# One core, an attention, channel-mixing and expert kernel: the order in which expert weights are fetched at the start of the expert stage

## The chip, the core and the metric

The kernel runs on one core of a Trainium2 chip. The metric is device microseconds of one execution. The core has five engines, each with its own in-order instruction stream: TensorE (PE in the profile, with its weight loads as PEld), VectorE (DVE), ScalarE (ACT), GpSimd (POOL) and SyncE (SP). SP computes nothing here; it issues the large transfers from DRAM, one after the other, and waits in between wherever a buffer is not free. The rows of gathered tokens and of results go through POOL's own transfer queue.

## What is computed

Three layers follow one another on 2 x 768 tokens of width 512: chunked attention with a few memory rows, a channel-mixing layer, and a mixture of 8 experts. The change touches the third alone. Cut to what matters:

```python
for b in range(B):
    prev_e = -1
    for s in range(S):
        fresh_e = int(np.argmax(logits[b, s]))
        e = fresh_e if s == 0 or local_gate[b, s] < 0.5 or prev_e < 0 else prev_e
        prev_e = e
        p = softmax(logits[b, s])
        h = np.maximum(x[b, s] @ w1[e], 0.0)      # w1: 8 x 512 x 1024
        out[b, s] = p[e] * (h @ w2[e])            # w2: 8 x 1024 x 512
```

Each token goes to one expert, and which one is known only on the chip. One expert's weights are two matrices of 2,048 KB each.

## The kernel before

**Slots.** The tokens of one expert are cut into full slots of 128 rows; what is left of an expert's tokens, if it is at most 64, becomes a half slot of 64 rows. Full slots run in order of their experts, numbered from 0; half slot h runs behind the full slot `HALF_AT[h]`, with `HALF_AT = (3, 5, 7, 8, 9, 11, 13, 15)`, so the first half slot stands behind full slot 3, which is the fourth, and the second behind full slot 5. With these inputs there are eleven full slots and five half slots. Full slots 0 to 3 belong to one expert, 4 to 7 to a second, 8 to a third, 9 and 10 to a fourth.

**Weights of full slots.** There is one raw buffer for them, `raw[0]`, in two halves: `raw[0][0]` for w1 and `raw[0][1]` for w2. `w_fetch(s, k)` (lines 848 to 855) has SP load half k of the next expert's weights into it when slot s is the first of an expert, and otherwise issues an empty load: the same instruction with a condition that is false. Either way it first reads two numbers of the table `nx` into SP's registers. `w_part(s, q)` (lines 835 to 846) turns a quarter of the raw weights into two lists of high and low parts: ACT writes the high part (line 830) and DVE subtracts it (line 833), four pieces each; it runs only if slot s is the first of its expert. For slot s + 1 its first two quarters run inside slot s, between the two middle parts of the second product (lines 1178 and 1180), the other two in slot s + 1 (lines 1161 and 1167).

**Weights of half slots.** They are used as they are, from `raw[1]` for half slots 0, 2, 4 and `raw[2]` for 1, 3, 5. `h_fetch(h)` (lines 1088 to 1096) reads two numbers of the table `ei` and issues two loads, r1 (line 1095) and r2 (line 1096). `half_end(h)` fetches for half slot h + 2 once half slot h has been computed.

**The order around the change.** Before slot 1, SP issues in this order (lines 1234 to 1238): a tiny transfer `mark`, which waits for the gather of slot 2; half slot 0's two loads; the second expert's two loads (`w_fetch(0, 0)` and `w_fetch(0, 1)`); half slot 1's two loads. Then come the `w_fetch` calls of slots 1 to 3: (2,0), (2,1), (3,0) and (3,1), which are empty here since slots 2 and 3 start no expert, and (4,0), which is a load of the third expert's w1 and needs `raw[0][0]` free. The framework makes every load, empty ones too, wait for the load that wrote the same half before it, and for its readers; and it makes a reader wait for the last load in program order, whether that was empty or not. So `w_part(4, 0)`, in slot 3, waits for the empty `w_fetch(3, 0)`.

**The first half slot.** On ACT the order in slot 3 is `w_part(4, 0)` (line 830), the high part of the next slot's transposed tokens (line 865), `w_part(4, 1)` (line 830), the scaling of slot 3's result `put` (line 909), and then half slot 0's first activation `h_relu(0)` (line 1121). On TensorE it is slot 3's last products, half slot 0's first product (line 1115), the transpose of its result (line 1128, which needs the activation of line 1121), the rest of the first product, the second product (line 1140, which needs r2), and slot 4's first product (line 882).

Of the kernel before, what the change touches and what calls it, by code (L numbers as in the profile page):

```python
# [143 lines left out]
def kernel(  # L144
# [692 lines left out]
    def w_part(s, part):  # L837
        if s < 2 or s >= NFULL:
            return
        k = (s, body[0] if s > NMIN and body[0] >= NMIN else 0)  # L840
        if k not in flag:
            flag[k] = nc.values_load(ei[0:1, 1, s:s + 1], engines=(ET.DVE, ET.Activation),
                                     min_val=0, max_val=1)
        with tc.If(flag[k]):  # L844
            for c in range(4):
                w_piece(s, part, c, nc.vector)

    def w_fetch(s, k):

        if s >= NFULL:  # L850
            return
        ev = nc.values_load(nx[0:1, 0, s:s + 1], engines=(ET.SP,), min_val=0, max_val=NE - 1)
        fv = nc.values_load(nx[0:1, 1, s:s + 1], engines=(ET.SP,), min_val=0, max_val=1)
        nc.sync.dma_start(out=raw[0][k], in_=(w1, w2)[k][bass.ds(ev, 1)].rearrange("o (c p) f -> p (o c) f", p=P),
                          cond=fv)

    def gather(s):
        if s >= NFULL:
            return
        rows = 1 + (NE_T * P if s < 2 else B * S)  # L860
        nc.gpsimd.indirect_dma_start(out=yg[s % 3], out_offset=None, in_=ys[0:rows, :],
                                     in_offset=bass.IndirectOffsetOnAxis(ap=gix[:, s:s + 1], axis=0))
# [5 lines left out]
    def tx(s):  # L868
        if s >= NFULL:
            return  # L870
        pb = banks[4]
        for c in range(NC):
            nc.tensor.transpose(pb[:, c * P:(c + 1) * P], yg[s % 3][:, c * P:(c + 1) * P], ident)
        split4(pb, *xbuf[s % 2])

    def s1(s, g, cs):
        xh, xl = xbuf[s % 2]
        pb = banks[g]
        for c in cs:
            wh, wl = w1_s[c][g]  # L880
            sl = slice(c * P, (c + 1) * P)
            nc.tensor.matmul(pb, lhsT=xh[:, sl], rhs=wh, start=(c == 0), stop=False)  # L882
            nc.tensor.matmul(pb, lhsT=xh[:, sl], rhs=wl, start=False, stop=False)  # L883
            nc.tensor.matmul(pb, lhsT=xl[:, sl], rhs=wh, start=False, stop=(c == NC - 1))  # L884

    def relu(s, g, on_act):
        if on_act:
            nc.scalar.activation(out=hv[g], in_=banks[g], func=ACTF.Relu)
        else:
            nc.vector.tensor_scalar(out=hv[g], in0=banks[g], scalar1=0.0, scalar2=None, op0=ALU.max)  # L890

    def th(s, g):
        pb = banks[5]
        for c in range(4):
            nc.tensor.transpose(pb[:, c * P:(c + 1) * P], hv[g][:, c * P:(c + 1) * P], ident)  # L895
        split4(pb, *hbuf[g])

    def s2(s, cs):
        pb = banks[2 + s % 2]
        for c in cs:  # L900
            hh, hl = hbuf[c // 4]
            wh, wl = w2_s[c]
            sl = slice((c % 4) * P, (c % 4 + 1) * P)
            nc.tensor.matmul(pb, lhsT=hh[:, sl], rhs=wh, start=(c == 0), stop=False)  # L904
            nc.tensor.matmul(pb, lhsT=hh[:, sl], rhs=wl, start=False, stop=False)  # L905
            nc.tensor.matmul(pb, lhsT=hl[:, sl], rhs=wh, start=False, stop=(c == NF - 1))  # L906

    def put(s):
        nc.scalar.activation(out=ot[0], in_=banks[2 + s % 2], func=ACTF.Copy, scale=yg[s % 3][:, DM:DM + 1])
        nc.vector.tensor_copy(sixl, six[:, s:s + 1])  # L910

    def store():

        nc.gpsimd.indirect_dma_start(out=out, out_offset=bass.IndirectOffsetOnAxis(ap=sixl, axis=0),  # L914
                                     in_=ot[0], in_offset=None, bounds_check=B * S - 1, oob_is_err=False)
# [172 lines left out]
    def h_fetch(h):  # L1088
        if h >= NE:
            return  # L1090
        s = NFULL + h
        ev = nc.values_load(ei[0:1, 0, s:s + 1], engines=(ET.SP,), min_val=0, max_val=NE - 1)
        fv = nc.values_load(ei[0:1, 1, s:s + 1], engines=(ET.SP,), min_val=0, max_val=1)
        r1, r2 = raw[1 + h % 2]
        nc.sync.dma_start(out=r1, in_=w1[bass.ds(ev, 1)].rearrange("o (c p) f -> p (o c) f", p=P), cond=fv)
        nc.sync.dma_start(out=r2, in_=w2[bass.ds(ev, 1)].rearrange("o (c p) f -> p (o c) f", p=P), cond=fv)
# [6 lines left out]
    def h_tx(h):  # L1103
        if h >= NE:
            return
        pb = banks[6]
        for c in range(NC):
            nc.tensor.transpose(pb[:, c * 64:(c + 1) * 64], yh[h % 2][0:64, c * P:(c + 1) * P], ident[0:64, 0:64])
        nc.scalar.activation(out=xh4[h % 2], in_=pb[:, 0:256], func=ACTF.Copy)
# [47 lines left out]
    def slot_body(s):  # L1157
        body[0] = s
        if s > 1:
            s1(s, 0, range(4))  # L1160
            w_part(s, 2)
            relu(s, 0, True)
        s1(s, 1, range(0, 2))
        th(s, 0)
        s1(s, 1, range(2, 4))
        relu(s, 1, False)
        w_part(s, 3)
        if s > 1:
            w_fetch(s, 1)
        if s - 1 not in HALF_AT:  # L1170
            store()
        gather(s + 2)
        s2(s, range(0, 2))
        if s in HALF_AT:
            h_tx(HALF_AT.index(s))
        th(s, 1)
        s2(s, range(2, 4))
        w_part(s + 1, 0)
        tx(s + 1)
        w_part(s + 1, 1)  # L1180
        if s > 0:
            w_fetch(s + 1, 0)
        s2(s, range(4, 8))
        put(s)

# [20 lines left out]
    def slots(s):  # L1206
        slot_body(s)
        if s == 1:
            h_gather(0)
            h_gather(1)  # L1210
            for k in range(2):
                nc.gpsimd.memset(oh[k], 0.0)
        if s in HALF_AT:
            with tc.If(nh > HALF_AT.index(s)):
                half_body(HALF_AT.index(s))
            store()
            half_end(HALF_AT.index(s))
        if s < NMIN - 1:
            slots(s + 1)
        elif s < NFULL - 1:  # L1220
            with tc.If(nv > s + 1):
                slots(s + 1)
# [9 lines left out]


    nc.sync.dma_start(out=mark, in_=yg[2][0:1, 0:1])
    h_fetch(0)
    w_fetch(0, 0)
    w_fetch(0, 1)
    h_fetch(1)
    slots(1)
    nr = nc.values_load(ei[0:1, 0, NSLOT + 2:NSLOT + 3], min_val=0, max_val=1)  # L1240
    with tc.If(nr):
# [83 lines left out]
```

## Time and profile before

| | us |
|---|---|
| median of 3 runs | 464.93 (464.39 to 465.23) |
| the profiled execution | 464.7 |
| its span in the trace | 462.9 |
| around the span | 1.8 |

The span is the time from the first to the last instruction of the program that the profiler saw. TensorE is busy for 90% of it. The expert stage with its slots runs from about 245 us to the end. In a timeline a row is a run of like instructions: its start, its length, engine and line, the operation with what it writes and reads, the number of instructions, and in square brackets how long the engine sat idle before it and what ended that. SPq marks instructions of SP; for a transfer the time is that of issuing it, not of moving it.

### The profile page before, as it was taken

Reading aid. Unit: us, or ns where it says so; the run is one execution under the profiler, and the core shown is the slowest. Engines: PE = TensorE matmul, PEld = TensorE weight load, DVE = VectorE, ACT = ScalarE, POOL = GpSimd, SP = SyncE. Lnnn points to the kernel's source line nnn. Section 1 sums busy time; section 2 is a strip of 40 time slices with the busy share of each in tenths; the row PEclk is TensorE's granted clock in tenths of the full one; section 3 lists DMA queues with packets and bytes.
Section 4 is the critical chain, followed back from the end, with each engine's and each line's share of the span. In section 5 each row is a group of like instructions: output and inputs, shape, how many; then the busy total and the mean of one; then the engine's idle time right before and its main releaser. Section 6 shows DMA issues by size and latency. Waiting matters only on the chain. (4 is left out here: it accounts for less than half of the span.)

```text
span 462.9 us, 10040 instructions
## 1 busy us (share of the span) xinstructions
PE 416.2 (90%) x3827; PEld 351.1 (76%) x3827; DVE 251.8 (54%) x637; ACT 186.8 (40%) x425; POOL 95.2 (21%) x98
## 2 busy tenths in 40 slices
PE   0557999999999999999999899994999999999992
PEld 0346899988999989998999678872686786767671
DVE  4999999735664476548622684214242116475210
ACT  3664995355420634214624212215332125465211
POOL 2312211422200221003313505110320210212020
PEclk9999999999999999999999999998899999999997
DMA  8979950224221120000750015999992850994010
GB/s 283 408 295 330 372 171 6 67 75 133 89 87 36 47 60 1 1 1 25 278 178 0 1 68 152 390 400 357 378 385 81 274 209 1 355 392 139 23 53 25
DMA packets 28099, 76.68 MB, mean 166 GB/s; under 512 B 3821, under 2 KB 3953, under 8 KB 28034
## 3 DMA queue, kind: packets, MB, share of 16 engines
q1 hardware_dynamic: 25218, 67.39, 40.1%
q0 software_dynamic: 2816, 8.47, 5.7%
q8 instruction: 34, 0.56, 0.5%
q14 instruction: 31, 0.25, 0.2%
HBM read 109.40 MB, written 6.69 MB: 251 GB/s over the span
## 5 line engine op out<-in xcount | busy, mean ns | idle before, releaser
L866 DVE TENSOR_TENSOR w<-bank,w 128x512 fp32r<-128x512 f32 x34 | 23.5, 690 | 72.8 <-ACTq L844 56.8
L212 POOL TENSOR_TENSOR k2l<-tmp,k2h 128x384 fp32r<-128x384 f32 x25 | 28.4, 1135 | 100.9 <-DVE k2h L209 63.8
L480 PE MATMUL bank<-xkh,w 128*128 128x384 f32 x128 | 46.6, 364 | 1.7 <-ACT tmp L500 1.6
L833 DVE TENSOR_TENSOR w<-raw,w 128x512 fp32r<-128x512 f32 x56 | 35.7, 696 | 19.7 <-ACT w L830 19.3
L481 PE MATMUL bank<-xkl,w 128*128 128x384 f32 x128 | 43.7, 341 | 1.0 <-DVE xkl L212 1.0
L480 PE MATMUL bank<-k2h,w 128*128 128x384 f32 x128 | 44.6, 349 | 0.0
L482 PE MATMUL bank<-xkh,w 128*128 128x384 f32 x128 | 43.7, 341 | 0.0
L482 PE MATMUL bank<-k2h,w 128*128 128x384 f32 x128 | 42.9, 335 | 0.0
L481 PE MATMUL bank<-k2l,w 128*128 128x384 f32 x128 | 42.8, 334 | 0.0
L865 ACT ACTIVATE w<-bank 128x512 fp32r<-128x512 f32 x34 | 20.3, 597 | 52.0 <-PE bank L895 27.8
L830 ACT ACTIVATE w<-raw 128x512 fp32r<-128x512 f32 x64 | 35.2, 621 | 8.2 <-DMA raw<-in_w_dram 8.2
L904 PE MATMUL bank<-w,w 128*128 128x512 f32 x88 | 36.3, 412 | 0.0
L882 PE MATMUL bank<-w,w 128*128 128x512 f32 x88 | 36.2, 412 | 0.0
L906 PE MATMUL bank<-w,w 128*128 128x512 f32 x88 | 34.6, 393 | 0.0
L883 PE MATMUL bank<-w,w 128*128 128x512 f32 x88 | 34.6, 393 | 0.0
L884 PE MATMUL bank<-w,w 128*128 128x512 f32 x88 | 34.6, 393 | 0.0
L905 PE MATMUL bank<-w,w 128*128 128x512 f32 x88 | 34.3, 390 | 0.0
L914 POOL DMA_INDIRECT out_dram<-ot,sixl x11 | 11.2, 1018 | 104.5 <-ACTq L844 29.5
L382 ACT ACTIVATE Pm<-bank,mx 128x64 f32<-128x64 f32 x96 | 21.3, 321 | 21.8 <-DVE mx L373 21.2
L506 ACT ACTIVATE tmp<-bank 128x384 f32<-128x384 f32 x24 | 11.9, 494 | 41.5 <-PE bank L482 38.9
L480 PEld LDWEIGHTS bank<-xkh,w 128*128 128x128 f32 x128 | 24.6, 192 | 4.7 <-ACT tmp L500 2.0
L481 PEld LDWEIGHTS bank<-xkl,w 128*128 128x128 f32 x128 | 24.6, 192 | 1.4 <-DVE xkl L212 1.4
(224 smaller groups left out, 916.7 us busy)
## 6 DMA issues: line engine op xcount, KB each, us to landing
raw<-in_w_dram SPq DMA_DIRECT2D x36, 2048.0 KB
qk<-in_qkx_dram SPq DMA_DIRECT2D x16, 576.0 KB
vt<-in_vx_dram SPq DMA_DIRECT2D x16, 390.0 KB
w<-in_wk_dram SPq DMA_DIRECT2D x8, 512.0 KB
w<-in_wv_dram SPq DMA_DIRECT2D x8, 512.0 KB
ys<-yr SPq DMA_DIRECT2D x12, 256.0 KB
w<-in_wr_dram SPq DMA_DIRECT2D x4, 512.0 KB
raw<-in_w_dram SPq DMA_DIRECT2D x2, 1024.0 KB
```

The source lines that it names most:

```text
L212: (nc.vector if e == "d" else nc.gpsimd).tensor_tensor(out=o, in0=a, in1=b, op=op)
L480: nc.tensor.matmul(o[:, :UT], lhsT=wh, rhs=xh, start=first, stop=False)
L481: nc.tensor.matmul(o[:, :UT], lhsT=wh, rhs=xl, start=False, stop=False)
L482: nc.tensor.matmul(o[:, :UT], lhsT=wl, rhs=xh, start=False, stop=last)
L830: nc.scalar.activation(out=hi, in_=src, func=ACTF.Copy)
L833: lo_on.tensor_tensor(out=lo, in0=src, in1=hi.bitcast(F32), op=ALU.subtract)
L882: nc.tensor.matmul(pb, lhsT=xh[:, sl], rhs=wh, start=(c == 0), stop=False)
L883: nc.tensor.matmul(pb, lhsT=xh[:, sl], rhs=wl, start=False, stop=False)
L884: nc.tensor.matmul(pb, lhsT=xl[:, sl], rhs=wh, start=False, stop=(c == NC - 1))
L904: nc.tensor.matmul(pb, lhsT=hh[:, sl], rhs=wh, start=(c == 0), stop=False)
L905: nc.tensor.matmul(pb, lhsT=hh[:, sl], rhs=wl, start=False, stop=False)
L906: nc.tensor.matmul(pb, lhsT=hl[:, sl], rhs=wh, start=False, stop=(c == NF - 1))
```

## The change

Before slot 1 the next expert's two loads are issued first and half slot 0's two behind them; half slot 1's two loads are not issued there any more. They are issued in slot 3, right behind `w_fetch(4, 0)`. No instruction of another engine changes, and the number of loads and their sizes stay the same.

```diff
@@ slot_body
         w_part(s + 1, 1)
         if s > 0:
             w_fetch(s + 1, 0)
+        if s == 3:
+            h_fetch(1)
         s2(s, range(4, 8))
         put(s)
@@ ahead of slot 1
     nc.sync.dma_start(out=mark, in_=yg[2][0:1, 0:1])
-    h_fetch(0)
     w_fetch(0, 0)
     w_fetch(0, 1)
-    h_fetch(1)
+    h_fetch(0)
     slots(1)
```

## Rows read from the trace of the kernel before

**Rows 1.** The page: busy time by engine, and the span in 40 equal slices.
```profile
PE 416.2 (90%) x3827; PEld 351.1 (76%) x3827; DVE 251.8 (54%) x637; ACT 186.8 (40%) x425; POOL 95.2 (21%) x98
PE   0557999999999999999999899994999999999992
```
**Rows 2.** Timeline of PE, half slot 0 to slot 4: start, length, engine, line.
```profile
313.40 2.81 PE L1115 MATMUL bank<-raw,xh 128*64 128x256 f32 x24
322.13 0.69 PE L1128 MATMUL bank<-ident,hv 128*128 128x128 f32 x2 [5.92 <-ACT hv L1121]
330.11 0.50 PE L882 MATMUL bank<-w,w 128*128 128x512 f32 x1
```
**Rows 3.** Timeline of ACT, slot 3 and half slot 0.
```profile
308.98 0.60 ACT L865 ACTIVATE w<-bank 128x512 fp32r<-128x512 f32 x1 [0.81 <-PE bank L895]
316.48 2.19 ACT L830 ACTIVATE w<-raw 128x512 fp32r<-128x512 f32 x4 [6.91 <-DMA raw<-in_w_dram]
...
321.70 0.37 ACT L1121 ACTIVATE hv<-bank 128x256 f32<-128x256 f32 x1
```
**Rows 4.** Timeline of SP (issues): the first loads, then the empty ones.
```profile
282.16 0.29 SPq L1234 DMA_DIRECT2D mark<-yg  x1
286.10 0.01 SPq L1095 DMA_DIRECT2D raw<-in_w_dram  x1
286.36 0.39 SPq L1096 DMA_DIRECT2D raw<-in_w_dram  x1
288.26 4.45 SPq L854 DMA_DIRECT2D raw<-in_w_dram  x1
...
314.28 0.08 SPq L854 DMA_DIRECT2D raw<-in_w_dram  x1
316.34 0.08 SPq L854 DMA_DIRECT2D raw<-in_w_dram  x1
...
322.78 0.38 SPq L854 DMA_DIRECT2D raw<-in_w_dram  x1
```
**Rows 5.** SP's waits, 306 to 316.5 us: total, times, longest.
```profile
SPq L854 <- DMA raw<-in_w_dram: 3.5, 1, 3.5
```
**Rows 6.** Stretches: length, busy time by engine, granted clock, DMA share, GB/s.
```profile
286.00:314.10 28.10, 27.63 (x139) 22.23 (x139) 5.53 (x10) 5.95 (x10) 3.98 (x4) 1.00 1.01 374
314.10:322.80 8.70, 2.78 (x24) 1.49 (x20) 5.57 (x10) 5.59 (x11) 0.00 (x0) 0.90 1.02 389
318.00:320.00 2.00, 0.00 (x0) 0.00 (x0) 2.00 (x4) 2.00 (x5) 0.00 (x0) 1.00 1.05 387
322.00:327.00 5.00, 4.87 (x22) 2.30 (x22) 1.14 (x4) 0.46 (x2) 1.02 (x1) 0.50 0.72 230
```
**Rows 7.** Timeline of PE, half slot 2, behind slot 7.
```profile
389.98 2.81 PE L1115 MATMUL bank<-raw,xh 128*64 128x256 f32 x24
392.72 0.44 PE L1128 MATMUL bank<-ident,hv 128*128 128x128 f32 x2
394.00 1.03 PE L1140 MATMUL bank<-raw,hh 128*64 128x256 f32 x8
398.07 0.50 PE L882 MATMUL bank<-w,w 128*128 128x512 f32 x1
```
**Rows 8.** Timeline of ACT, slot 7 and half slot 2; one row of slot 8.
```profile
386.09 2.20 ACT L830 ACTIVATE w<-raw 128x512 fp32r<-128x512 f32 x4
...
392.03 0.39 ACT L1121 ACTIVATE hv<-bank 128x256 f32<-128x256 f32 x1 [0.61 <-PE bank L1115]
...
398.62 2.20 ACT L830 ACTIVATE w<-raw 128x512 fp32r<-128x512 f32 x4
```
**Rows 9.** Timeline of DVE: the table `nx`; the low parts in slot 7.
```profile
276.12 0.15 DVE L1047 CAST nx<-tmp 1x17 int32<-1x17 f32 x1
390.12 2.48 DVE L833 TENSOR_TENSOR w<-raw,w 128x512 fp32r<-128x512 f32 x4
```
**Rows 10.** Timeline of PE, the start of half slot 1.
```profile
356.02 2.81 PE L1115 MATMUL bank<-raw,xh 128*64 128x256 f32 x24
```

## The prediction

> **What bounds the kernel now.** I read the page first: TensorE is busy for 90% of the span, and in the row of 40 slices it stands at 9 from the fourth or fifth slice to the end, but for one slice of 4, the 28th (312 to 324 us), one of 8 and the last [rows 1]. So the expert stage is bound by TensorE, and the one hole is worth a look of its own. The timeline of PE shows it: the first product of half slot 0 starts at 313.40, and the transpose behind it at 322.13, after 5.92 us idle that ended with ACT's activation of line 1121 [rows 2]. Then the timeline of ACT tells why that came late. ACT was done with slot 3's previous piece at 308.98 + 0.60 = 309.58, stood idle for 6.91 us until a load into `raw`, and then did, in its order, w_part(4, 0) from 316.48, the rest, and the activation at 321.70, ended 322.07 [rows 3]. That is 5.59 us of ACT work behind the wait, and half slot 0's activation is queued behind all of it, though it needs nothing of it.
>
> Which load was it? The order of issues on SP answers: the third `w_fetch` of the empty ones, (3, 0), goes out at 316.34, and ACT starts 0.14 us later [rows 3, 4]. It was late because the one before it, (2, 1), had to wait for the load that wrote `raw[0][1]` before it: SP waited 3.5 us for a transfer [rows 5] and issued (2, 1) at 314.28 and (3, 0) 2.06 us later [rows 4]. The load that it waited for is `w_fetch(0, 1)`, fourth in SP's queue, which therefore landed at about 314.1. From the first issue at 286.10 that is 28.0 us for four loads [rows 4], 7.0 us each, at 374 GB/s with the gathers and stores in between [rows 6].
>
> **What the change removes.** Without the wait, slot 3 and half slot 0 should look like slot 7 and half slot 2, where the same instructions run in the same order with w_part(8, 0) and (8, 1) in front of the activation. There ACT starts w_part at 386.09, 3.89 us before PE's first product at 389.98; the same distance from 313.40 is 309.51, when ACT is free in slot 3 too [rows 3, 7, 8]. There the transpose starts 2.74 us after the first product and slot 8 follows 8.09 us after it [rows 7]. In slot 3 these are 8.73 and 16.71 us [rows 2]. So 16.71 - 8.09 = **8.62 us** go: 5.99 of stall, and 2.63 of slow clock behind it. [...]
>
> **When the new order releases w_part(4, 0).** `nx` is written at 276.12 [rows 9], before `mark` goes out at 282.16 [rows 4], so the table is no new wait. From the end of one issue to a `w_fetch`'s own it takes 288.26 - 286.75 = 1.51 us to read the two numbers [rows 4]. The first load of the new order, `w_fetch(0, 0)`, can go out at 282.45 + 1.51 = 284.0; at the latest I take 286.3, if whatever held SP until 286.10 holds it again. `w_fetch(0, 1)` is now second instead of fourth: landed after 2 x 7.0 = 14.0 us, at 298.0 to 300.3; were the second to land only when three have their share, 21 us after the first issue, 307.3. Add 2.06 us for (3, 0): w_part(4, 0) is released at 300.1 to 302.4, and at 309.4 by the far bound. ACT comes to it at 309.5. In half slot 2 ACT had 0.61 us to spare before its activation [rows 8], so up to 310.1 costs nothing, and each us later costs one us. Even the far bound costs nothing; I take 0.
>
> **Half slot 0's own loads, moved behind two others.** r1 is now third and r2 fourth. The fourth landed 28.0 us after the first issue, so r2 lands at 312.0 to 314.3 and r1 one load of about 5.6 us (2.10 MB at 374 GB/s [rows 6]) earlier, at 306.4 to 308.7. r1 is read from 313.40 on; r2 by line 1140, which starts 4.02 us after the first product [rows 7], at 317.4. That leaves 4.7 to 7.0 and 3.1 to 5.4 us. PE's work hides both loads; if that cover is gone, each us costs one us. I take 0, and 1 us as the high end, since no row shows a single load's own landing but the fourth's.
>
> **Half slot 1's loads, moved past the slots.** On SP they now stand behind the wait of `w_fetch(4, 0)` for w_part(4, 1), which ended with DVE's subtractions in the old order (issue at 322.78 [rows 4]). In slot 7 the subtractions end at 390.12 + 2.48 = 392.60, 2.62 us after the first product [rows 7, 9]; so `w_fetch(4, 0)` goes out at about 316.1, and the two numbers of `ei` and r1, r2 of half slot 1 behind it from 317.6. Queued behind them on SP are the two loads for half slot 2, `w_fetch(4, 1)` and the empty ones of slot 5. At 7.0 us each half slot 1's second load lands 21 us after 316.1, at 337. Half slot 1 starts at 356.02 [rows 10], less 8.62 = 347.4: 10 us to spare. `w_fetch(4, 1)` is sixth: 42 us, 358, and its reader, w_part(8, 2), comes at 398.62 [rows 8] less 8.62 = 390.0. The queue moves as many bytes as before. I take 0 for this step. [...] Here the rows say that 10 us of earliness are left.
>
> **The sum.** Against the profiled execution 464.7 - 8.6 = 456.1; its run lies 0.2 below the median of the three, so the median should be 464.93 - 8.62 = **456.3 us**. Behind slot 4 the order on every engine is as it was, and PE stays the bound, so nothing gives it back. Below 8.62 us there is little to gain further: slot 3's own products already run without a gap to 313.4.
>
> **The rivals.**
> Empty loads that queue. If an empty load's signal came only behind all loads ahead of it in the queue, (3, 0) would land behind half slot 0's r2, at 312.0 to 314.3. ACT's chain would end 5.59 us later, at 317.6 to 319.9, instead of by 316.1: 1.5 to 3.8 us of stall stay. Gone would be the rest, 457.8 to 460.1 us. Against it: ACT started 0.14 us after the issue at 316.34 while the queue still moved 389 GB/s [rows 3, 4, 6]. [...] The trace shows no such wait for an empty load. Chance 0.06.
>
> Half slot 0's loads late, a little. If r2 lands 1 to 2 us behind its reader, 457.3 to 458.3. Chance 0.07.
>
> Half slot 0's loads late, much: the other side. PE would now wait at line 1115 for r1, which was first in the queue and is third. For a loss, the stall and its clock must exceed 8.62 us, so r1 must land after about 313.4 + 6.0 = 319.4, that is 33 us after the first issue, where the old order needed 28.0 for four loads. It could be if SP is held ahead of `h_fetch(0)`, whose buffers lie in memory that earlier tiles used and which waits for their readers. It issued at 286.10, though, so these were free by then. If it decides, 465.5 to 468. Chance 0.04.
>
> The change does not reach the wait: ACT is held by something that the order of loads does not move, and half slot 0 stalls as before, 464.9. Against it is the chain of issues above. Chance 0.03.
>
> **How the numbers follow.** Forecast 0.80, own range 455.6 to 457.0: both ends of the loads' bounds and the spread of the three runs, 0.4 us to a side. The range takes in the small lateness of half slot 0's loads: 455.4 to 458.3, which holds 0.87 by these chances. 0.2% of the time, 0.9 us, is about what a measurement of this kernel can tell from no change. Faster by more than that: 0.80 + 0.06 + 0.07 = 0.93; within it 0.03; slower 0.04.
>
> **What would show it.** In the changed kernel's timeline line 1128 of half slot 0 starts 2.7 us after line 1115 with no idle time before it, and slot 4 follows 8.1 us after; the granted clock stays 1.00 from 313 to 330; ACT starts w_part(4, 0) at about 309.5 with no wait for a load; (3, 0) is issued by 305; half slot 1 starts at about 347.4 without waiting. If line 1115 or 1140 waits for a load, the step on half slot 0's loads was wrong; if ACT waits at line 830, the one on the release; if line 1115 of half slot 1 waits, the one on its loads. A later wait of PE that was not there before would make the sum wrong.

## The result, and the profile after

The changed kernel takes 456.30 us (median of 4 executions, 456.02 to 456.43), the kernel before 464.69 us on the same chip (464.39 to 465.23). The ratio is 0.9817, with a 95% interval of 0.9800 to 0.9834. The forecast was 456.3 us.

The page of the changed kernel, busy time by engine and the 40 slices. TensorE works for 2 us less, in a span that is 8.3 us shorter (454.6 us), and the slice of 4 is gone:

```profile
PE 414.2 (91%) x3827; PEld 350.9 (77%) x3827; DVE 252.0 (55%) x637; ACT 187.0 (41%) x425; POOL 94.4 (21%) x98
...
PE   0557999999999999999999999999999999999992
```

The timeline of PE answers to [rows 2]: half slot 0, its transpose, its second product and slot 4, then half slot 1, which answers to [rows 10].

```profile
313.70 2.81 PE L1115 MATMUL bank<-raw,xh 128*64 128x256 f32 x24
316.44 0.44 PE L1128 MATMUL bank<-ident,hv 128*128 128x128 f32 x2
...
317.72 1.03 PE L1140 MATMUL bank<-raw,hh 128*64 128x256 f32 x8
...
321.80 0.50 PE L882 MATMUL bank<-w,w 128*128 128x512 f32 x1
...
347.70 2.81 PE L1115 MATMUL bank<-raw,xh 128*64 128x256 f32 x24
```

The transpose has no idle time in brackets any more; it starts 2.74 us after the first product, and slot 4 follows 8.10 us after it, where it was 16.71 us. That is 8.61 us. (Half slot 0 itself starts 0.30 us later than before, a drift from stages that the change does not touch: `mark` goes out at 282.48 instead of 282.16. So the span differs by 8.3.) From the start of slot 4 to the end of the span it takes 132.8 us in both kernels: 462.9 - 330.11 and 454.6 - 321.80. The whole gain lies in half slot 0.

The timeline of ACT answers to [rows 3]. w_part(4, 0) (line 830) starts at 309.79 with no wait, and the activation of line 1121 now waits 0.64 us for PE, as it does in half slot 2 [rows 8], instead of PE for it:

```profile
309.28 0.60 ACT L865 ACTIVATE w<-bank 128x512 fp32r<-128x512 f32 x1 [0.81 <-PE bank L895]
309.79 2.19 ACT L830 ACTIVATE w<-raw 128x512 fp32r<-128x512 f32 x4
...
315.75 0.39 ACT L1121 ACTIVATE hv<-bank 128x256 f32<-128x256 f32 x1 [0.64 <-PE bank L1115]
```

The timeline of SP answers to [rows 4]: the second expert's two loads, half slot 0's two, the empty loads (2, 0), (2, 1), (3, 0), then `w_fetch(4, 0)` and half slot 1's two. The wait in front of (2, 1), for the landing of `w_fetch(0, 1)`, is there as before [rows 5]; it ends at 302 instead of 314:

```profile
284.44 0.45 SPq L854 DMA_DIRECT2D raw<-in_w_dram  x1
286.73 0.39 SPq L854 DMA_DIRECT2D raw<-in_w_dram  x1
288.80 4.00 SPq L1095 DMA_DIRECT2D raw<-in_w_dram  x1
293.10 2.62 SPq L1096 DMA_DIRECT2D raw<-in_w_dram  x1
297.27 0.09 SPq L854 DMA_DIRECT2D raw<-in_w_dram  x1
302.12 0.08 SPq L854 DMA_DIRECT2D raw<-in_w_dram  x1
303.73 0.07 SPq L854 DMA_DIRECT2D raw<-in_w_dram  x1
...
316.42 0.38 SPq L854 DMA_DIRECT2D raw<-in_w_dram  x1
318.44 0.21 SPq L1095 DMA_DIRECT2D raw<-in_w_dram  x1
318.94 0.50 SPq L1096 DMA_DIRECT2D raw<-in_w_dram  x1
```

SP's wait between 298 and 304 us (total, times, longest):

```profile
SPq L854 <- DMA raw<-in_w_dram: 3.3, 1, 3.3
```

Stretches of the changed kernel, with the columns of [rows 6]: the last columns are the granted clock, the share of the transfer engines and GB/s. The clock stays at 1.00 through half slot 0, and the queue runs dry before 314 us (0.02 of the transfer engines' time from 313 to 314), so half slot 0's second load, the last of the four, was there nearly 4 us ahead of line 1140 at 317.72:

```profile
313.00:314.00 1.00, 1.00 (x8) 0.53 (x8) 1.00 (x3) 1.00 (x3) 0.00 (x0) 1.00 0.02 8
...
313.00:330.00 17.00, 17.00 (x112) 11.88 (x111) 9.36 (x18) 8.89 (x18) 3.98 (x4) 1.00 0.74 274
```

### The profile page after: what moved, and what is told of

Same layout as the page of the kernel before. It is cut to its first block, busy times and chain, and to the rows that moved or that the text cites. A ratio compares the mean times of both kernels' runs of the same rounds, so it can differ in the third digit from the quotient of the medians.

```text
span 454.6 us, 10038 instructions
## 1 busy us (share of the span) xinstructions
PE 414.2 (91%) x3827; PEld 350.9 (77%) x3827; DVE 252.0 (55%) x637; ACT 187.0 (41%) x425; POOL 94.4 (21%) x98
## 5 line engine op out<-in xcount | busy, mean ns | idle before, releaser
L212 POOL TENSOR_TENSOR k2l<-tmp,k2h 128x384 fp32r<-128x384 f32 x25 | 27.1, 1085 | 100.9 <-DVE k2h L209 63.8
L506 ACT ACTIVATE tmp<-bank 128x384 f32<-128x384 f32 x24 | 11.8, 494 | 41.5 <-PE bank L482 38.9
```

Source lines behind the costliest of these rows:

```text
L212: (nc.vector if e == "d" else nc.gpsimd).tensor_tensor(out=o, in0=a, in1=b, op=op)
```

## The experiments

The theory: ACT waited in w_part(4, 0) because the empty load (3, 0), on which it waits, is issued behind (2, 1), and that one waits for the landing of `w_fetch(0, 1)`; the new order lets this landing come 12 us earlier. The rivals: it is the bytes ahead in the queue, or only the order, or the place of half slot 1's loads, that count.

### Only the later issue of half slot 1's loads

```diff
     h_fetch(0)
     w_fetch(0, 0)
     w_fetch(0, 1)
-    h_fetch(1)
     slots(1)
...
+        if s == 3:
+            h_fetch(1)
```

> One half of the change alone: half slot 0's loads stay first and the second expert's behind them; half slot 1's loads move to slot 3. Theory (the release of w_part(4, 0) goes through the chain of empty loads, whose second waits for the landing of w_fetch(0, 1)): w_fetch(0, 1) is still fourth and lands about 28 us after the first issue, at 314; the empty (3, 0) goes out 2.06 us later, at about 316; ACT's wait of 6.9 us stays, and so does the time, 464.7 us within 0.5. Rival (the 4 MB of half slot 1 in the queue ahead of the empty loads hold them up): with them gone w_part(4, 0) is released by about 310 and most of the gain is there, 456 to 458 us.

Measured: 464.18 us against 464.59, ratio 0.9994 (0.9979 to 1.0008). No change clear of noise. SP's timeline has (2, 1) at 314.09 and (3, 0) at 315.70, although 4 MB fewer lie ahead of them in the queue, and ACT's w_part(4, 0) starts 0.14 us after (3, 0):

```profile
314.09 0.08 SPq L854 DMA_DIRECT2D raw<-in_w_dram  x1
315.70 0.07 SPq L854 DMA_DIRECT2D raw<-in_w_dram  x1
```
```profile
315.84 2.19 ACT L830 ACTIVATE w<-raw 128x512 fp32r<-128x512 f32 x4 [6.08 <-DMA raw<-in_w_dram]
```

SP's wait between 309 and 315 us (total, times, longest) is the one in front of (2, 1), for the landing of `w_fetch(0, 1)`:

```profile
SPq L854 <- DMA raw<-in_w_dram: 4.3, 1, 4.3
```

The 4 MB behind the second expert's loads were not what held ACT; the landing of `w_fetch(0, 1)`, still fourth, was. This half of the change alone is worth nothing that can be told from noise (0.4 us by the medians).

### Only the new order

```diff
-    h_fetch(0)
     w_fetch(0, 0)
     w_fetch(0, 1)
+    h_fetch(0)
     h_fetch(1)
     slots(1)
```

> The other half alone: the second expert's loads first, half slot 0's behind them, and half slot 1's still ahead of slot 1. Theory: w_fetch(0, 1) lands at about 302, so the empty loads no longer wait for it; but SP issues them one after the other behind the sixth load, whose issue ended at 307.5 in the kernel before and ends 0 to 1.7 us earlier here. From there (2, 0), (2, 1) and (3, 0) take 1.5, 1.6 and 1.6 to 2.0 us: (3, 0) at 310.6 to 312.7. ACT may start up to 310.4 at no cost, so 0.3 to 2.5 us of stall stay, with no fall of the granted clock: 456.6 to 458.8 us. Rival (the order is all that counts): 456.3 us, as with the whole change. Rival (the 4 MB must land first): 464 us.

Measured: 459.89 us, ratio 0.9893 (0.9862 to 0.9924), 1.1 us above the range of the theory. The mechanism was right: the issue of the fifth load holds SP for 6.58 us and that of the sixth for 3.19, until 304.09 + 3.19 = 307.28, and behind it the empty ones, (3, 0) at 312.53, inside the 310.6 to 312.7 that were expected:

```profile
297.23 6.58 SPq L1095 DMA_DIRECT2D raw<-in_w_dram  x1
304.09 3.19 SPq L1096 DMA_DIRECT2D raw<-in_w_dram  x1
308.83 0.09 SPq L854 DMA_DIRECT2D raw<-in_w_dram  x1
310.52 0.08 SPq L854 DMA_DIRECT2D raw<-in_w_dram  x1
312.53 0.08 SPq L854 DMA_DIRECT2D raw<-in_w_dram  x1
```

ACT's w_part(4, 0) starts 0.14 us behind it, at 312.67:

```profile
312.67 2.19 ACT L830 ACTIVATE w<-raw 128x512 fp32r<-128x512 f32 x4 [3.06 <-DMA raw<-in_w_dram]
```

The size was not, because the clock fell all the same. The timeline of PE and the stretches of this kernel:

```profile
313.44 2.81 PE L1115 MATMUL bank<-raw,xh 128*64 128x256 f32 x24
318.32 0.44 PE L1128 MATMUL bank<-ident,hv 128*128 128x128 f32 x2 [2.08 <-ACT hv L1121]
...
325.26 0.50 PE L882 MATMUL bank<-w,w 128*128 128x512 f32 x1
```
```profile
313.00:319.00 6.00, 3.92 (x33) 2.16 (x33) 5.57 (x10) 5.47 (x12) 0.00 (x0) 1.00 1.03 400
319.00:320.00 1.00, 1.00 (x12) 0.63 (x10) 0.18 (x1) 0.18 (x1) 0.28 (x1) 0.86 1.03 379
320.00:323.00 3.00, 3.00 (x16) 1.35 (x14) 0.67 (x2) 0.00 (x0) 0.73 (x1) 0.50 1.05 389
```

The transpose comes 4.88 us after the first product, 2.14 more than without a stall; from there to slot 4 it takes 6.94 us instead of 5.36. So 2.14 us of stall drew 1.58 us of slow clock after it, 3.72 us together; the medians of this kernel and the changed one differ by 3.6. Both halves of the change are needed for its whole gain: the order lets `w_fetch(0, 1)` land early, and taking half slot 1's loads away lets SP reach the empty loads early.

### The old order without the empty loads of slots 2 and 3

```diff
     def w_fetch(s, k):
-        if s >= NFULL:
+        if s >= NFULL or s in (2, 3):
             return
```

> The kernel before, in its old order of loads, without the empty loads of slots 2 and 3 (which start no expert with these inputs, so that nothing is moved by them; a kernel that left them out would not do for other inputs). Theory: w_part(4, 0) then waits for w_fetch(0, 0) itself, third in the queue, landed about 21 to 23 us after the first issue, 307 to 309; ACT needs it at 309.5, so the stall is gone with no load moved: 456.3 us within 0.6. Rival (the bytes ahead of the second expert's weights cost the time, not the chain of empty loads): 464 to 465 us, as before.

Measured: 456.21 us, ratio 0.9820 (0.9795 to 0.9846), the whole gain with no load moved. ACT's waits of 306 to 318 us hold none for a load any more (total, times, longest):

```profile
ACT xh L1109 <- PE bank L1108: 2.5, 1, 2.5
ACT w L865 <- PE bank L895: 1.9, 2, 1.1
ACT hh L1130 <- PE bank L1128: 0.8, 1, 0.8
ACT hv L1121 <- PE bank L1115: 0.6, 1, 0.6
```

Half slot 0 runs as in the changed kernel: its first product starts at 314.42, the transpose 2.74 us later and slot 4 8.10 us later.

This is the run that settles the cause. All six loads go out in the old order. The weights that w_part(4, 0) needs were there in time also in the kernel before: by the trace's records of the loads' signals `w_fetch(0, 0)` landed at 308.9 there, and ACT was free at 309.58 [rows 3]. What was late was the permission to read them, which hung on a load that moves nothing.

### Both

```diff
     def w_fetch(s, k):
-        if s >= NFULL:
+        if s >= NFULL or s in (2, 3):
             return
...
     w_fetch(0, 0)
     w_fetch(0, 1)
     h_fetch(0)
     slots(1)
```

> The changed kernel without the empty loads of slots 2 and 3 (which move nothing with these inputs). Theory: the new order and leaving out the empty loads take away the same wait, and nothing is left of it in the changed kernel, so that the two do not add up: 456.3 us within 0.5. Rival (they take away different waits): 2 us or more below 456.3.

Measured: 456.42 us, ratio 0.9827 (0.9795 to 0.9859). The two do not add up: they remove one wait, in two ways.

### Half slot 1's loads ahead of half slot 0's

```diff
-    h_fetch(0)
     w_fetch(0, 0)
     w_fetch(0, 1)
     h_fetch(1)
+    h_fetch(0)
     slots(1)
```

> The second expert's loads first, half slot 1's behind them and half slot 0's last, all ahead of slot 1. It takes away the cover of half slot 0's loads. Theory: its first load is fifth and lands about 33 us after the first issue, at 318; TensorE waits for it in front of line 1115 from 313.7, 4 us; its second lands at 323, 1.2 us after its reader. So 5.2 us of stall, each us one us: 461.5 us if the granted clock stays, and 2.6 more, 464.1, if it falls to half as it did in the kernel before. Rival (the loads share the queue, so that the order hardly matters): 456 to 459 us.

Measured: 464.49 us, ratio 1.0001 (0.9984 to 1.0017). The wait that the change removed is replaced by another one of nearly the same price, now of PE for the load itself:

```profile
319.36 4.99 PE L1115 MATMUL bank<-raw,xh 128*64 128x256 f32 x24 [5.60 <-DMA raw<-in_w_dram]
```

The stretches of this kernel show the clock already at half when the products begin:

```profile
313.00:317.00 4.00, 0.77 (x4) 0.30 (x2) 4.00 (x8) 4.00 (x9) 0.00 (x0) 1.00 1.02 408
317.00:323.00 6.00, 3.64 (x18) 2.13 (x20) 1.31 (x4) 0.40 (x1) 1.02 (x1) 0.50 1.05 391
```

Half slot 0 takes from 319.36 to slot 4 at 329.64, 10.28 us, 2.18 more than at full clock; with the 5.60 us of wait, 7.8 us. The load landed 1.3 us later than expected (319.3 instead of 318), and its second one just in time, so that its 1.2 us did not come.

All six loads stand ahead of the empty ones here, as with only the new order, so ACT waits for (3, 0) too. That wait ends at 312.07, 0.14 us after the issue of (3, 0) at 311.93, and ACT has done the work queued ahead of the activation at 317.4, before the products begin, so it is not what this run pays for:

```profile
312.07 2.19 ACT L830 ACTIVATE w<-raw 128x512 fp32r<-128x512 f32 x4 [2.20 <-DMA raw<-in_w_dram]
```

The order of issue decided when this load landed, at 319.3 as the fifth here and at 307.7 as the third in the changed kernel, and with that whether the gain was there.

### Half slot 1's loads one slot later

```diff
-        if s == 3:
+        if s == 4:
             h_fetch(1)
```

> The changed kernel with half slot 1's loads one slot later still, in slot 4 behind w_fetch(5, 0), so behind half slot 2's loads and w_fetch(4, 1) in the queue. It takes away the 10 us that the moved step had to spare. Theory: they become fifth and sixth of the loads that begin at 316.4; in the changed kernel those landed at 350.3 and 356.4. Half slot 1's first product would wait from 348.0 to 350.3 and its second from 354.3 to 356.4, 4.4 us in all: 460.7 us, up to 463 if the granted clock falls too. Rival (the place of these loads does not matter as long as they are ahead of half slot 1): 456.3 us.

Measured: 461.11 us, ratio 0.9930 (0.9903 to 0.9957), 4.8 us above the changed kernel. PE waits for both loads, and the granted clock falls once more, from 1.00 until 350 to 0.64 from 350 to 352 and 0.51 from 352 to 354 (1.68 us longer to the transpose than the usual 2.74):

```profile
350.25 4.50 PE L1115 MATMUL bank<-raw,xh 128*64 128x256 f32 x24 [2.61 <-DMA raw<-in_w_dram]
354.67 0.44 PE L1128 MATMUL bank<-ident,hv 128*128 128x128 f32 x2
...
356.43 1.08 PE L1140 MATMUL bank<-raw,hh 128*64 128x256 f32 x8 [0.30 <-DMA raw<-in_w_dram]
...
360.55 0.50 PE L882 MATMUL bank<-w,w 128*128 128x512 f32 x1
```

So the moved step is free because of the time that it has to spare, not by itself: one slot later and the spare time is used up.

### A wait that is left: the half slots' transposes

```diff
+        if s in HALF_AT:
+            h_tx(HALF_AT.index(s))
         s2(s, range(0, 2))
-        if s in HALF_AT:
-            h_tx(HALF_AT.index(s))
         th(s, 1)
```

> The changed kernel with the transposes of the half slot's tokens (line 1108) ahead of the two middle parts of slot s's second product, by six products earlier, in the five slots that a half slot follows. In the changed kernel TensorE waits 0.47 us there behind line 1108 for ACT's copy of line 1109, five times, 2.4 us. Theory: the copy then ends under the six products, 1.4 us, and the wait is gone: 453.9 us. Rival (another wait of the transposes of line 895 takes its place, the activation or bank 5): 456.3 us.

Measured: 454.53 us, ratio to the kernel before 0.9775 (0.9746 to 0.9804). Its five executions (453.50 to 454.77) all lie below those of the kernel with both edits on the same chip (456.24 to 456.57). This is the fastest version. The row for the wait, from the changed kernel's list of PE's waits, is gone from this kernel's:

```profile
PE bank L895 <- ACT xh L1109: 2.4, 5, 0.5
```

By the medians it brings 1.8 us against the changed kernel and 1.9 against the kernel with both edits, not 2.4. From half slot 0's first product to half slot 4's it takes 425.05 - 313.70 = 111.35 us in the changed kernel and 423.15 - 313.19 = 109.96 here, 1.39 us for four of the five waits, 0.35 each. In slot 3 the wait of 0.47 us is gone, but line 1108 now starts 0.43 us after the product in front of it, where it was 0.32; that accounts for most of the difference, and why it is so stays open.

## Why the prediction was right, point by point

**The size of the gain.** The comparison with half slot 2 gave 8.62 us; the trace has 8.61 (16.71 to 8.10). Of these 5.99 lie ahead of the transpose (8.73 to 2.74) and 2.62 behind it, where PE takes 7.98 us to slot 4 in the kernel before, at a granted clock of 0.50 from 322 to 327 [rows 2, 6], and 5.36 at 1.00 in the changed kernel. The median moved by 8.39, from 464.69; the 464.93 that the forecast was counted from, a median of three, was 0.24 higher. That the forecast is met to the digit is luck: from 464.69 it would have been 456.07, and the 0.30 us by which half slot 0 starts later in the changed kernel's profile was not foreseen either.

**The release of w_part(4, 0).** Forecast 300.1 to 302.4, with 309.4 as the far bound; (3, 0) went out at 303.73, 1.3 us past the likely end. The first issue came near its early end, at 284.44 for 284.0; what was mis-sized is the landing of `w_fetch(0, 1)`, 17.5 us after the first issue and not 14.0. A mean of 7.0 us a load was too plain a rule: by the records of the loads' signals the four landed 11.8, 17.5, 23.3 and 29.2 us after the first issue, so the first took 11.8 us and each one behind it 5.7 to 6.0. The 6 us between the release and ACT's start at 309.79 hid the miss. The theory of the wait itself stands on three runs: fewer bytes in the queue do nothing, an earlier landing alone gives 4.7 of the 8.4 us, and without the empty loads all of it is there.

**Half slot 0's loads.** Forecast 306.4 to 308.7 and 312.0 to 314.3; by the same records 307.7 and 313.7. Their readers came at 313.70 and 317.72, so 6.0 and 4.1 us were left.

**Half slot 1's loads.** Forecast 337 for the second; the records say 338.5, against half slot 1's start at 347.70: 9 us to spare instead of 10. `w_fetch(4, 1)` was forecast for 358 and landed at 356.4. One slot later costs 4.8 us, so the margin was real and not wide.

**The rival of the empty loads that queue.** ACT starts 0.14 us after the issue of (3, 0) in all four kernels in which it waits for it: the kernel before, and those with only the later issue, with only the new order, and with half slot 1's loads first. In all but the second of these the queue moved 389 to 408 GB/s meanwhile. In the changed kernel ACT does not wait for it at all. The signal of a load whose condition is false did not wait for the loads ahead of it: in the kernel before half slot 1's two, issued ahead of (3, 0), landed at 319.4 and 324.6 by the records of the loads' signals, and ACT started at 316.48 [rows 3]. The four loads that move something landed in the order of their issue in the changed kernel, at 296.2, 302.0, 307.7 and 313.7.

**The rival on the other side.** It was put at a landing of half slot 0's first load after 319.4, as the point from which the change would lose. The run with half slot 1's loads first moved that landing to 319.3, and the time came out even with the kernel before, 1.0001. The point was right to what these runs can tell.

**What was mis-sized.** For small lateness the prediction took "each us costs one us". The runs deny it: 2.1 us of stall cost 3.7 with only the new order, and 2.9 us (2.61 and 0.30) cost 4.8 with half slot 1's loads a slot later, since the granted clock fell each time, to 0.50 and to 0.51. By an estimate from these two, the stalls of about 2 us and more in the rival of the queueing empty loads and in that of the late loads would have cost 1.6 to 2 us more than was put down. What a stall of 1 us costs is not shown: no run has one of that length in a half slot. It did not touch the forecast, which had no stall, but the upper end of the range, 458.3, was too low for the 2 us of late loads that it claimed to hold; with a stall of 2.1 us the time was 459.89.

**What was misread.** The prediction says that slot 3's own products already run without a gap, so that little is left to gain. In the kernel before they have one, the same that the last experiment takes away:

```profile
308.22 0.66 PE L895 MATMUL bank<-ident,hv 128*128 128x128 f32 x4 [0.47 <-ACT xh L1109]
```

The forecast does not hang on it, since the change leaves this wait as it is.

## What to carry to other kernels

When an engine waits for a transfer, look at which issue it hangs on, not at the bytes: here it was an empty one, and what it waited for was the previous write of the same buffer, for which SP stood 3.5 us [rows 5] with its next issues behind it. What a stall of TensorE costs, the slow clock behind it included, can be read off a twin stage of the same trace that has no stall: here half slot 2 gave 8.62 us, and 8.61 went. A load that is moved later is free only as long as its reader is further away than all that was put in front of it; one slot more took 4.8 us.

## What the runs showed of the hardware

Behind a stall of 2.1 us the granted clock fell to 0.50, and the fall came after TensorE had begun again. In the kernel with only the new order PE stopped for 2.08 us and began again at 318.32; the granted clock was 1.00 until 319, 0.86 in the next us and 0.50 from 320 to 323, with PE busy all the while. In the kernel before it stood still for 5.92 us and began again at 322.13 [rows 2]; the clock was 1.00 until 320, 0.99 in the next us and 0.50 from 321 to 327. The slow clock cost 1.6 us behind the stall of 2.1, about 1.7 behind that of 2.6, 2.7 behind that of 5.1 (the kernel with only the later issue), 2.2 behind that of 5.6 and 2.6 behind that of 5.9: over these five it grew much less than the stall, and not in step with it. Behind the stall of 5.6 the clock stood at 0.50 from 317 already, 2.4 us before the products began at 319.36, so less of the slow stretch fell on work.

With two or more loads under way, most of the issues of loads that move something held SP longer. The first two 2,048 KB loads of the changed kernel were issued in 0.45 and 0.39 us, the third and fourth behind them held SP for 4.00 and 2.62 us, and the fifth and sixth of the kernel with only the new order for 6.58 and 3.19; in slot 3 of the changed kernel the third took 0.50 us, and the fourth, at 321.31, 5.49. The fifth and sixth hold SP for 9.8 us ahead of the empty loads; the later issue of half slot 1's loads takes that out of their way.
